# Second pass of a forward Fourier transform: each matmul of 128 rows and 192 columns against two of 64 rows and 96 columns

## The chip, the cores and the metric

The kernel runs on one core of one Trainium2 chip, as one launch. The metric is the device time of that core in microseconds (us). Columns, rows and loads below are those of TensorE, the matrix engine: a matmul first loads its stationary operand (the weights) into the array of 128 by 128 cells, as an instruction of its own, and then streams the columns of its moving operand through it; sums arrive in PSUM.

## The reference

The input x has 4 batches of 3072 positions with 256 features, all float32. Three layers follow one another:

```python
X = rfft(x, axis=1)                               # 1537 frequencies
Yr = Xr @ w_r - Xi @ w_i + b_r
Yi = Xr @ w_i + Xi @ w_r + b_i
Y  = soft threshold of Yr and of Yi at 0.01
y  = irfft(Y)                                     # "Fourier"
xk, xr = mixes of y with y one position earlier
y  = sigmoid(xr @ w_r2) * (relu(xk @ w_k)**2 @ w_v)  # 256 -> 1024 -> 256
h  = y @ w_in                                     # 256 -> 2048
out = (h * tanh(softplus(h))) @ w_out             # 2048 -> 256
```

The change lies in the first line, the forward transform.

## The kernel before, in words

**Precision.** TensorE works on float32r operands here. For float32 accuracy every operand is split in two parts, a high one (written by a copy with rounding, on ScalarE) and a low one (the difference, on VectorE); `split`, L71 to L77, does both, so that the casts of many tiles are recorded at L76 and the differences at L77. A product is then three matmuls into one PSUM group: high by high, high by low, low by high.

**Forward transform.** 3072 is taken as 96 by 32. The first pass, `s1` (L256 to L269), sums over 96 with weights `FC` of 96 by 96 and goes through DRAM (`scr1`), which turns the data. The second pass, `s2` (L298 to L310), sums over 32. Real and imaginary part of 32 positions are 64 rows, so a group of 128 rows holds two independent sums of 64 rows, s = 0 and s = 1, and the constant matrix `MC` (128 rows, 192 columns: minus imaginary, real, imaginary, 64 columns of each) is block diagonal: in each of its three parts of 64 columns the rows 0 to 63 have values in the first 32 columns only, and the rows 64 to 127 in the last 32 only.

**A unit of work.** There are 48 units u, 12 a batch (`NU`, `NG`). A unit has 2 groups e of 128 rows, and 256 features, which as two halves dh of 128 are the weights' columns: `s2(u)` issues 2 x 2 x 3 = 12 matmuls, each with a weight load of 128 rows by 128 columns out of `Ah` or `Al`, and 192 moving columns of `MC`. The output tile `s2p` has two banks of PSUM, one for each e, and there is one buffer of it. `s2_ev(u)` (L317 to L335) splits it into `Xh` and `Xl` in SBUF, 768 elements in each of 128 partitions (ScalarE L76, VectorE L77). `mix(u)` (L339 to L361) multiplies these with the layer's weights in 24 matmuls of 256 columns, adds the bias and applies the threshold on VectorE (L358 to L360). `is1(u)` (L369 to L379) is the first pass of the inverse transform, 3 matmuls of 512 columns (6 of 256 in four units).

**Order.** The program is ordered by hand; each engine carries out its instructions in the order written. The loop at L620 issues in turn u: `s2(u + 2)`, its eviction `s2_ev(u + 2)`, with `split_Y(u - 1)`, evictions of the first pass and two steps of background work (`bg`: splitting of later weights, mostly on VectorE) after it; the load of unit u + 5 from `scr1` (SP's queue) and the split of unit u + 4 into `Ah` and `Al`; the copy of the inverse pass's result (L388, to DRAM `scr2` by SP's queue); `mix(u)`; in 20 of the turns 12 matmuls of the first pass of a later batch; and `is1(u - 2)`. On TensorE a turn is thus: second pass, mix, first pass at times, inverse pass. From u = 33 on the next layer begins beside it (`early`, with matmuls of 96 rows and 128 columns, L458).

After this stage come the gated layer (from L819) and the last layer (from L1063), which the change does not touch.

Of the kernel before, what the change touches and what calls it, by code (L numbers as in the profile page):

```python
# [29 lines left out]
def kernel(  # L30
# [27 lines left out]
    nc = tc.nc  # L58
# [12 lines left out]
    def split(src, hi, lo, lo_eng=None, hi_eng=None):  # L71

        if hi_eng is nc.vector:
            nc.vector.tensor_copy(out=hi, in_=src)
        else:
            nc.scalar.copy(out=hi, in_=src)  # L76
        (lo_eng or nc.vector).tensor_tensor(out=lo, in0=src, in1=hi, op=ALU.subtract)  # L77
# [220 lines left out]
    def s2(u):  # L298
        last = u % NG == GS
        hl = Ah.pop(u)  # L300
        p = ps1p.tile([128, 2, 512], F32, tag="s2", name="s2p", bufs=1)
        for e in range(2):
            mc = MC[:, int(last and e == 1)]
            for dh in range(2):
                for i, (a, w) in enumerate(((0, 0), (0, 1), (1, 0))):
                    nc.tensor.matmul(  # L306
                        out=p[:, e, dh * 192:(dh + 1) * 192], lhsT=hl[a][:, e, dh * 128:(dh + 1) * 128],
                        rhs=mc[:, w, :], start=(i == 0), stop=(i == 2),
                    )
        s2_t[u] = p  # L310

    S1_AT = {2 + i: 4 + i for i in range(4)}
# [4 lines left out]
    def s2_ev(u, fill=lambda: None):  # L317
        last = u % NG == GS
        p = s2_t.pop(u)

        v = p[:, :, 0:384].rearrange("p e (h c) -> p e h c", h=2)
        xh = p1p.tile([128, 2, 2, 192], F32R, tag="Xh", name="Xh", bufs=3)
        xl = p1p.tile([128, 2, 2, 192], F32R, tag="Xl", name="Xl", bufs=3)
        split(v, xh, xl)
        fill()
        Xh[u] = (xh, xl)
        if last:

            xb = p1p.tile([128, 2, 2, 128], F32R, tag="Xb", name="Xb", bufs=1)
            for k, v in enumerate((xh, xl)):  # L330
                nc.scalar.copy(out=xb[:, k], in_=v[:, 1, :, 0:128])
            nc.scalar.activation(
                out=xb[:, :, :, 32:128:64], in_=xb[:, :, :, 32:128:64], func=AF.Copy, scale=0.0
            )
            Xb[u] = xb  # L335
# [204 lines left out]
    split_A(0)  # L540
    split_A(1)
    s2(0)
    s1(1, 2)
    split_mix(1)
    split_x(1, 3)
    s2_ev(0)
    s1_ev()
    s1_ev()
    s2(1)
    s1(1, 3)  # L550
    split_W()
    split_A(2)
    load_A(4)
    s2_ev(1)
    load_x(1, 5)
    split_x(1, 4)
# [6 lines left out]
    for h in range(2):  # L563
        for q in range(2):
            cs = slice(q * 512, (q + 1) * 512)
# [54 lines left out]
    for u in range(NU + 3):  # L620
        if u + 2 < NU:
            s2(u + 2)
# [3 lines left out]
        def fill():  # L626
            if 1 <= u <= NU:
                split_Y(u - 1)
            while s1_t:
                s1_ev()  # L630
            if u > 2:
                bg(2)

        if u + 2 < NU:
            s2_ev(u + 2, fill)
        else:
            fill()
# [11 lines left out]
        if u in S1_AT:  # L649
            i = 8 + S1_AT[u]  # L650
# [33 lines left out]
    for q in range(4):  # L684
        for h in range(2):
            cs = slice(q * 512, (q + 1) * 512)
# [132 lines left out]
    for t in range(NA + 1):  # L819
# [5 lines left out]
        for i2 in range(4):  # L825
# [48 lines left out]
            if t == NA - 1 and i2 == 0:  # L874
                hl = x2h_t[0] = w2p.tile([128, 2, 2, 512], F32R, tag="x2h", name="x2h", bufs=1)
# [292 lines left out]
```

## Time and profile before

| | us |
|---|---|
| median of 2 runs | 2007.81 (2006.71 to 2008.91) |
| span of the profiled execution | 2006.0 |
| TensorE busy in it | 1974.4 |
| VectorE busy | 1534.1 |
| ScalarE busy | 1149.5 |

The profiled execution's own time is its span, from the first to the last instruction; it lies 1.81 us under the median of the runs. The second pass runs from 37.6 to 301.6 us of it, 48 units, 576 matmuls. A matmul's recorded duration reaches from its start to its modelled end, and matmuls overlap in the pipeline: the pace is read from start to start. In a row of the timeline, "x2" with 0.36 us is two instructions of one group, from the start of the first to the end of the second.

### The profile page before, as it was taken

What the parts mean: (1) busy time and instruction counts of PE and PEld (TensorE: products, weight loads), DVE (VectorE), ACT (ScalarE), POOL (GpSimd) and SP (SyncE); (2) the same over time, 40 slices, a digit from 0 to 9 for tenths busy, and PEclk for the clock granted to TensorE, in tenths of its full rate; (3) what the DMA queues carried; (4) which work ended last, traced back from release to release, by engine and by line L of the source; (5) the groups of instructions that cost most, each with busy time, mean ns of one, the idle gap of its engine ahead of it and who ended that gap; (6) DMA issues with size and microseconds to landing.
All of it is one profiled execution on the core that took longest, in us unless ns stands there. A gap on an engine that the chain in (4) does not pass through costs nothing.

```text
span 2006.0 us, 33418 instructions
## 1 busy us (share of the span) xinstructions
PE 1974.4 (98%) x13284; PEld 1890.9 (94%) x13284; DVE 1534.1 (76%) x2487; ACT 1149.5 (57%) x1703; POOL 28.1 (1%) x45
## 2 busy tenths in 40 slices
PE   6999999999999999999999999999999999999998
PEld 5999999999999999999989999999999999999997
DVE  6899997777776776775587778777787777877775
ACT  6666656777777777776544444444444444544443
POOL 0000000000000000000000000000000000000000
PEclk8999999999999999999999999999999999999999
DMA  8676532112121211111101000001010010000000
GB/s 265 181 214 201 168 111 90 53 58 70 49 80 49 65 62 58 60 49 46 37 22 32 22 25 30 22 22 33 22 33 22 22 33 22 28 27 22 22 12 22
DMA packets 71501, 123.19 MB, mean 61 GB/s; under 512 B 6192, under 2 KB 48432, under 8 KB 71344
## 3 DMA queue, kind: packets, MB, share of 16 engines
q1 hardware_dynamic: 67200, 106.49, 18.0%
q0 software_dynamic: 4144, 14.55, 1.9%
q8 instruction: 105, 1.72, 0.4%
q14 instruction: 52, 0.43, 0.1%
HBM read 70.69 MB, written 50.33 MB: 60 GB/s over the span
## 4 chain that ended last, share of the span: by engine, by line
PE 91%; DVE 4%; DMA 2%; ACT 1%; issue 1%; SPq 0%; DVEq 0%; ACTq 0%
PE h L992 20%; PE o L1040 17%; PE kp L766 13%; PE vp L804 13%; PE o L1041 9%; PE mxp L352 5%; PE p L992 3%; PE pp L743 3%; PE pp L458 3%; PE s2p L306 2%; PE s1p L265 1%; PE i1p L376 1%; DMA XS<-in_x_dram 1%; DMA A<-scr 1%; DVE Xl L77 1%
## 5 line engine op out<-in xcount | busy, mean ns | idle before, releaser
L1040 PE MATMUL o<-WO,gh 128*128 128x512 f32 x1536 | 562.5, 395 | 0.0
L1041 PE MATMUL o<-WO,gl 128*128 128x256 f32 x1536 | 430.5, 280 | 0.0
L992 PE MATMUL h<-xS,WS 128*128 128x256 f32 x2208 | 351.6, 281 | 0.0
L1005 ACT COPY p1s<-p 128x256 f32<-128x256 f32 x184 | 68.9, 374 | 470.9 <-PE p L992 469.9
L1040 PEld LDWEIGHTS o<-WO,gh 128*128 128x128 f32 x1536 | 289.1, 188 | 43.3
L992 PEld LDWEIGHTS h<-xS,WS 128*128 128x128 f32 x2208 | 300.4, 189 | 16.1
L766 PE MATMUL kp<-xk,WK 128*128 128x384 f32 x1536 | 291.3, 338 | 0.3 <-DVE yT L474 0.3
L1041 PEld LDWEIGHTS o<-WO,gl 128*128 128x128 f32 x1536 | 289.8, 189 | 0.2
L804 PE MATMUL vp<-kh,WV 128*128 128x384 f32 x1024 | 281.7, 336 | 0.0
L766 PEld LDWEIGHTS kp<-xk,WK 128*128 128x128 f32 x1536 | 267.5, 189 | 0.8 <-ACT Cs L388 0.8
L995 DVE TENSOR_TENSOR C<-h,p1s 128x512 f32<-128x512 f32 x184 | 127.2, 691 | 161.7 <-PE h L992 161.7
L791 DVE TENSOR_TENSOR kl<-kr,kh 128x768 fp32r<-128x768 f32 x128 | 122.9, 960 | 163.6 <-ACT kr L790 163.3
L977 DVE TENSOR_TENSOR gl<-g,gh 128x1024 fp32r<-128x1024 f32 x184 | 223.7, 1216 | 2.1 <-ACT g L974 2.1
L973 ACT ACTIVATE gh<-C 128x1024 fp32r<-128x1024 f32 x184 | 195.7, 1063 | 11.0 <-DVE C L995 11.0
L974 ACT ACTIVATE g<-C 128x1024 f32<-128x1024 f32 x184 | 193.0, 1049 | 0.0
L992 PE MATMUL h<-xS,WI 128*128 128x256 f32 x1104 | 190.4, 280 | 0.0
L995 DVE TENSOR_TENSOR C<-h,wu 128x512 f32<-128x512 f32 x368 | 187.6, 552 | 0.1
L804 PEld LDWEIGHTS vp<-kh,WV 128*128 128x128 f32 x1024 | 186.7, 188 | 0.0
L804 PE MATMUL vp<-kl,WV 128*128 128x384 f32 x512 | 171.7, 335 | 0.0
L789 ACT ACTIVATE kh<-kr 128x768 fp32r<-128x768 f32 x128 | 108.4, 847 | 88.0 <-PE vp L804 87.9
L992 PEld LDWEIGHTS h<-xS,WI 128*128 128x128 f32 x1104 | 156.0, 189 | 0.2 <-DVE xS L953 0.2
L995 DVE TENSOR_TENSOR wu<-h,C 128x512 f32<-128x512 f32 x184 | 126.6, 688 | 35.0 <-PE h L992 31.1
(152 smaller groups left out, 3136.7 us busy)
## 6 DMA issues: line engine op xcount, KB each, us to landing
A<-scr SPq DMA_DIRECT2D x48, 256.0 KB
scr<-Cs SPq DMA_DIRECT2D x48, 256.0 KB
D<-scr SPq DMA_DIRECT2D x32, 384.0 KB
x2d<-r POOLq DMA_DIRECT2D x32, 384.0 KB, 3.5
x<-x2d SPq DMA_DIRECT2D x24, 512.0 KB
out_dram<-ob SPq DMA_DIRECT2D x96, 128.0 KB
scr<-st SPq DMA_DIRECT2D x27, 384.0 KB
xs<-in_x_dram SPq DMA_DIRECT2D x24, 384.0 KB
```

Of the source, the lines that this page charges most:

```text
L352: nc.tensor.matmul(out=p[:, e, :], lhsT=a, rhs=WX[:, dh, c, w, :], start=(i == 0), stop=(i == 11))
L766: nc.tensor.matmul(out=p[:, m, 0:TA], lhsT=WK[:, dh, w, f * 128:(f + 1) * 128], rhs=hl[:, v, dh, :], start=(i == 0), stop=(i == 5),)
L789: nc.scalar.activation(out=kh, in_=kr, func=AF.Square)
L791: nc.vector.tensor_tensor(out=kl, in0=kr, in1=kh, op=ALU.subtract)
L804: nc.tensor.matmul(out=p[:, o, 0:TA], lhsT=WV[:, f, w, o * 128:(o + 1) * 128], rhs=v[:, m, :], start=(f == 0 and i == 0), stop=(f == 7 and ...
L973: nc.scalar.activation(out=gh, in_=c, func=AF.Mish)
L974: nc.scalar.activation(out=g, in_=c, func=AF.Mish)
L977: nc.vector.tensor_tensor(out=gl, in0=g, in1=gh, op=ALU.subtract)
L992: nc.tensor.matmul(out=out, lhsT=a(l), rhs=xS[:, v, b, :], start=(n == 0), stop=(n == 2))
L995: nc.vector.tensor_tensor(out=out, in0=x0, in1=x1, op=ALU.add)
L1040: nc.tensor.matmul(out=o[m], lhsT=gh[:, m2, ms], rhs=WO[:, f], start=(f == 0), stop=False)
L1041: nc.tensor.matmul(out=o[m][:, 0, :], lhsT=gl[:, m2, ms], rhs=WO[:, f, 0, :], start=False, stop=(f == 15))
```

## The change

Each of the 12 matmuls of a unit becomes two. Matmul s takes rows 64 s to 64 s + 63 of the same weights (128 columns as before) and of `MC`, and from `MC` only the 96 columns in which those rows have values: 32 of each of the three parts, that is three runs of 32 with a step of 64. It thus lies in one half of the array's rows. The output of half s goes to bank s of `s2p` (before: bank e), with columns 192 e + 96 dh on. So the tile's order is now (s, then e, dh, part, 32 columns), and the eviction reads it back in the old order, 12 times 2 runs of 32, alternating between the banks. `Xh` and `Xl` and all that follows have the old layout. Values that are left out of the sums are products with zeros.

```diff
--- before.py
+++ after.py
@@ -303,10 +303,13 @@
             mc = MC[:, int(last and e == 1)]
             for dh in range(2):
                 for i, (a, w) in enumerate(((0, 0), (0, 1), (1, 0))):
-                    nc.tensor.matmul(
-                        out=p[:, e, dh * 192:(dh + 1) * 192], lhsT=hl[a][:, e, dh * 128:(dh + 1) * 128],
-                        rhs=mc[:, w, :], start=(i == 0), stop=(i == 2),
-                    )
+                    for s in range(2):
+                        rs, cs = slice(64 * s, 64 * s + 64), slice(192 * e + 96 * dh, 192 * e + 96 * dh + 96)
+                        nc.tensor.matmul(
+                            out=p[:, s, cs], lhsT=hl[a][rs, e, dh * 128:(dh + 1) * 128],
+                            rhs=mc[rs, w, :].rearrange("p (c s j) -> p c s j", c=3, s=2)[:, :, s, :],
+                            start=(i == 0), stop=(i == 2),
+                        )
         s2_t[u] = p
 
     S1_AT = {2 + i: 4 + i for i in range(4)}
@@ -318,10 +321,10 @@
         last = u % NG == GS
         p = s2_t.pop(u)
 
-        v = p[:, :, 0:384].rearrange("p e (h c) -> p e h c", h=2)
+        v = p[:, :, 0:384].rearrange("p s (c j) -> p c s j", c=12)
         xh = p1p.tile([128, 2, 2, 192], F32R, tag="Xh", name="Xh", bufs=3)
         xl = p1p.tile([128, 2, 2, 192], F32R, tag="Xl", name="Xl", bufs=3)
-        split(v, xh, xl)
+        split(v, *(a.rearrange("p e h (c s j) -> p (e h c) s j", c=3, s=2) for a in (xh, xl)))
         fill()
         Xh[u] = (xh, xl)
         if last:
```

## Rows read from the trace of the kernel before

**Rows 1.** The page: engines' busy time and share, instructions; a DMA queue: packets, MB, share.
```profile
span 2006.0 us, 33418 instructions
...
PE 1974.4 (98%) x13284; PEld 1890.9 (94%) x13284; DVE 1534.1 (76%) x2487; ACT 1149.5 (57%) x1703; POOL 28.1 (1%) x45
...
q8 instruction: 105, 1.72, 0.4%
```

**Rows 2.** The chain of waits, 0 to 400 us: share by line.
```profile
by line: PE mxp L352 23.9%; PE s2p L306 11.3%; PE s1p L265 7.2%; PE kp L766 7.2%; PE vp L804 6.0%; PE i1p L376 5.3%; DMA XS<-in_x_dram 3.4%; issue 2.9%; DMA A<-scr 2.6%; DVE Xl L77 2.5%; DMA xs<-in_x_dram 2.5%; DVE Al L77 2.3%; DVE yt L358 
```

**Rows 3.** Table by stretches: busy (instructions) of each engine, granted clock, DMA share, GB/s.
```profile
50.00:250.00 200.00, 200.00 (x1619) 195.93 (x1619) 188.16 (x293) 127.46 (x218) 0.00 (x0) 1.00 0.65 192
250.00:300.00 50.00, 48.24 (x377) 45.50 (x375) 48.25 (x88) 27.77 (x51) 0.00 (x0) 1.00 0.36 109
```

**Rows 4.** Timeline, matmuls, 155.3 to 157.3 us: start, duration, what, count.
```profile
155.61 0.36 PE L306 MATMUL s2p<-MC,Ah 128*128 128x192 f32 x2
155.81 0.28 PE L306 MATMUL s2p<-MC,Al 128*128 128x192 f32 x1
...
156.26 0.38 PE L306 MATMUL s2p<-MC,Ah 128*128 128x192 f32 x2
...
156.93 0.42 PE L352 MATMUL mxp<-WX,Xh 128*128 128x256 f32 x2
```

**Rows 5.** Timeline, weight loads of the same unit.
```profile
155.72 0.19 PEld L306 LDWEIGHTS s2p<-MC,Al 128*128 128x128 f32 x1
155.84 0.30 PEld L306 LDWEIGHTS s2p<-MC,Ah 128*128 128x128 f32 x2
...
156.84 0.30 PEld L352 LDWEIGHTS mxp<-WX,Xh 128*128 128x128 f32 x2
```

**Rows 6.** Timeline, weight loads, the unit at half clock; nine loads between these starts.
```profile
38.97 0.55 PEld L306 LDWEIGHTS s2p<-MC,Ah 128*128 128x128 f32 x2
...
40.89 0.28 PEld L265 LDWEIGHTS s1p<-xh,FC 96*96 96x96 f32 x1
```

**Rows 7.** Timeline, weight loads of the first pass: 22 us; and 153 us, after mix.
```profile
22.55 0.16 PEld L265 LDWEIGHTS s1p<-xh,FC 96*96 96x96 f32 x1 [0.79 <-ACT xh L76]
22.64 0.16 PEld L265 LDWEIGHTS s1p<-xl,FC 96*96 96x96 f32 x1
...
153.39 0.17 PEld L265 LDWEIGHTS s1p<-xh,FC 96*96 96x96 f32 x1
153.51 0.16 PEld L265 LDWEIGHTS s1p<-xl,FC 96*96 96x96 f32 x1
```

**Rows 8.** Groups by shape, 45 to 320 us: rows*columns, count, busy, mean ns, idle before.
```profile
L306 PEld LDWEIGHTS s2p<-MC,Ah 128*128 128x128 f32 x368 | 58.0, 191 | 7.4 <-DVE Xl L77 4.6
...
L77 DVE TENSOR_TENSOR Xl<-s2p,Xh 128x768 fp32r<-128x768 f32 x47 | 44.7, 952 | 4.3 <-ACT Xh L76 4.1
...
L265 PEld LDWEIGHTS s1p<-xh,FC 96*96 96x96 f32 x165 | 24.0, 162 | 0.0
...
L458 PEld LDWEIGHTS s1p<-ifh,Dl 96*128 96x128 f32 x16 | 3.1, 192 | 0.2
```

**Rows 9.** Timeline, matmuls, a unit that began after a wait.
```profile
250.98 0.47 PE L306 MATMUL s2p<-MC,Ah 128*128 128x192 f32 x2 [0.44 <-DVE Xl L77]
```

**Rows 10.** Groups by line, 0 to 700 us and 45 to 320 us: additions from PSUM.
```profile
L474 DVE TENSOR_TENSOR yT<-ya,pp 128x128 f32<-128x128 f32 x108 | 24.3, 281 | 0.0
...
L474 DVE TENSOR_TENSOR yT<-ya,s1p 128x64 f32<-128x64 f32 x24 | 3.7, 216 | 0.2 <-ACT ya L471 0.2
```

**Rows 11.** Waits, 0 to 320 us: us in total, times, longest.
```profile
ACT Xh L76 <- PE s2p L306: 71.6, 45, 3.4
```

**Rows 12.** Waits, 45 to 360 us, as above.
```profile
PEld s2p L306 <- DVE Xl L77: 4.6, 7, 0.9
```

## The prediction, made before the changed kernel was run

> **What bounds the kernel now.** I read the page first. TensorE is busy for nearly the whole span, while the lines of VectorE and ScalarE stay below it [rows 1]: a change on TensorE must be priced on TensorE. The chain of waits, cut to the first 400 us, shows who sets the end in the stage that holds the change: the matmuls of mix lead, those of the second pass (L306) stand second with 11.3%, and VectorE and DMA have a few per cent each [rows 2]. The table by stretches says the same of the steady part: between 50 and 250 us TensorE is busy without a break, at the full clock, and VectorE comes close to it; from 250 to 300 us TensorE lacks 1.8 us of 50 [rows 3]. So until 250 us every us added to TensorE's stream is added to the time, and later a few can vanish in gaps.
>
> Then the question is what a matmul of the second pass costs there, and the timeline answers it. The matmuls of a unit go by in about 0.11 us each, though 192 columns need less: the first two of a unit, whose weights were ready, last 0.36 us together where one lasts 0.28, so they follow one another in 0.08 to 0.09 us; a later pair takes 0.38 [rows 4]. The weight loads show why. From the third of the unit (155.72) to the first of mix (156.84) there are ten, in 1.12 us: **0.112 us each**, back to back [rows 5]. At half clock the same loads take 1.92/9 = 0.213 us each (38.97 to 40.89) [rows 6], and loads of 96 columns follow one another in 0.08 to 0.09 us where they run freely (22.55, 22.64) [rows 7]. The pace goes with the clock and with the number of weight columns. This pass is held by its **weight loads**, not by the columns that stream through.
>
> **The change, part by part.** *Streaming.* A matmul's 192 columns become two of 96, which may run beside each other. By the pace of the free pair, 0.085 us for 192 columns, that is 0.04 us for 96. But it was not the limit: worth nothing as long as a load takes 0.112 us.
>
> *Weight loads.* Each of the 12 loads of a unit becomes two, and each has 128 columns still; only its rows are halved. Do rows count? A load of 96 rows and 128 columns takes 192 ns, one of 128 rows and 128 columns 191, one of 96 by 96 162 [rows 8]: columns count, rows don't. The Trainium skill says so too (TensorE: Matmul & The Clock Gate, LDWEIGHTS): a load's time goes by its columns and not by the contraction rows; the trace agrees with the rows just named. So 12 loads more a unit. The trace has no load into half of the rows, and what a pair costs is bounded from two sides. One after another: 12 x 0.112 = 1.34 us a unit, 48 units, **64.5 us**. At the same time, in the two halves: nothing. A gain would need a load that is shorter for its fewer rows, which the 96-row loads speak against. I take the upper end: every load in the trace, whatever its shape, starts after its predecessor at the pace of its columns, and none starts beside another. One unit runs at half clock [rows 6]: 12 x (0.213 - 0.112) = 1.2 us more.
>
> *Issue.* The unit's 24 instructions on TensorE become 48. Their dispatch is not seen alone; 12 loads and 12 matmuls go by in the 1.32 us from 155.61 to 156.93 [rows 4], so one costs 0.055 us or less. At nothing it adds nothing. At that bound, 24 more cost 1.32 us, the price of the loads again, and not on top of it. A second way to the same sum.
>
> *Entering and leaving the half-array layout*, twice a unit, 96 times. The trace shows no such switch; between 96-row and 128-row instructions the loads go on without a pause (153.39 and 153.51) [rows 7], which gives zero for the lower end. The upper end is a full stop: the tail of a matmul beyond its slot, 0.27 - 0.11 = 0.16 us, and a weight load that nothing covers, 0.11, together 0.27 us, 26 us in all. The nearest row is a unit that began after a wait: its first two matmuls last 0.47 us [rows 9] instead of 0.36 [rows 4], 0.11 us for starting with no weights ready. I take that: 96 x 0.11 = **10.6 us**. The Trainium skill (TensorEngine Tiling, Key Properties) has a rule against this change: a switch of tiling mode drains TensorE. No run here shows it yet; by it the switches would cost up to the 26 us, without it nothing.
>
> *The evictions.* ScalarE's Xh and VectorE's Xl now read runs of 32 elements from two banks in turn. Additions that read PSUM in runs of 32 take 216 ns for 64 elements and 281 for 128 [rows 10], 1.02 ns an element, so 768 would be 0.93 us against the 952 ns of Xl now [rows 8]: no cost to be seen. A loss here is covered as well: ScalarE idles 71.6 us in all ahead of Xh, 45 times, waiting for the pass [rows 11], and the next unit needs the tile only after mix, some 3 us later. That s2p is one buffer matters only where VectorE is late.
>
> *What a later end of the pass sets back.* Behind Xh on ScalarE are queued Yh, the copies of st and Cs and the splits; behind Xl on VectorE are Yl and Al. All of them feed TensorE one or two units later, and TensorE itself is late by the same amount, so no new wait arises. No DMA is added or moved past another on SP's or POOL's queue; their triggers only come later with ScalarE's copies. The additional instructions, 1152 beside 33418, are 3% of a queue that takes 0.4% of the DMA engines [rows 1]: nothing.
>
> *What the gaps give back.* In the steady part TensorE's loads of this pass wait 4.6 us in 7 places for VectorE's Xl [rows 12]. VectorE gains 1.34 us a unit on TensorE, so these waits go: -4.6 us.
>
> **Sum:** 64.5 + 1.2 + 10.6 - 4.6 = +71.7 us. The profiled execution has a span of 2006.0 us; the median of the runs, 2007.8, is 1.8 us above it. 2006.0 + 71.7 + 1.8 = **2079 us**, +3.6%. With both ends of the switch cost (0 and 26 us), and 0 to 7 us given back, this case spans 2066 to 2096.
>
> **Rivals.** *The halves load side by side.* If the load into rows 64 to 127 starts while the one into rows 0 to 63 is under way, a pair takes the slot that one takes now, and the pass stays at 1.34 us a unit. The price is then the switches alone: 2008 us without one, 2018 with 0.11 us each, 2034 at the full stop: not slower by more than 2%. It decides at the second load of a pair: the loss falls below 40 us as soon as its start-to-start is less than half of 0.112 us, switches at my price. Against it: no two loads overlap in that way in this trace. For it: no load here names half of the rows, so the trace could not show it. The Trainium skill (TensorEngine Tiling, Key Properties) states this rule: tiles are independent, and different ones can load weights and multiply in parallel; no run here shows it yet. Chance 0.41.
>
> *Halved outright.* If a load into 64 rows cost half, or the halves hid each other's loads wholly, the pass would be held by streaming, 12 x 0.04 us beside each other: 0.83 us less a unit, 40 us, 1968 us; one half of that, 1988, is more believable. Against it are the loads of 96 rows. The Trainium skill (TensorEngine Tiling, Theoretical Speedup) gives up to 2x for a contraction of 64 or less; by that the pass would save 32 us. Nothing in this trace supports it for a pass held by weight loads. Chance 0.03.
>
> *The change does not take effect*: the 64-row matmuls occupy the whole array and run in a row. Then streaming adds nothing either, as 0.04 us stays under a load's 0.112: the forecast's 64.5 us without the switches, 2068. It lies within the forecast.
>
> **How the numbers follow.** Forecast, two slots for a pair, be it by loading or by dispatch: 0.56. Side by side 0.41, halved 0.03. About 2% (40 us, to 2048 or 1968) is what a measurement of this kernel can tell from no change. The forecast's case lies wholly above 2048, the second wholly within, the third almost wholly within: faster 0.01, within 2% 0.43, slower 0.56. The range must reach to the second case: 2008 to 2096 leaves out its lowest end, the third case and a switch dearer than a full stop, together some 0.15. The forecast's own range is 2066 to 2096.
>
> **What would show it.** In the changed kernel's timeline of weight loads, the second load of a pair starts 0.11 us after the first (forecast) or within some 0.06 us (side by side). A unit of the pass takes 2.7 us or 1.3 to 1.6. At the last matmul of is1 and the first of mix a pause of 0 to 0.27 us tells the switch. Xl should stay near 0.95 us, and the waits of loads for Xl should be gone. The prediction is wrong if the loads of the two halves overlap, if a load of 64 rows is clearly shorter than 191 ns, if the evictions slow down by tenths of a us, or if the clock of this stage falls below 1.00.

## The result and the profile after

The changed kernel takes 2023.1 us (2022.1 to 2024.2) against 2007.8, a ratio of **1.008** (95% interval 1.0064 to 1.0096). Run again beside the later experiments it took 2024.4 against 2007.3 (1.0086, 1.0072 to 1.0099). It is slower by 15 to 17 us, not by the 71 us of the forecast; the rival "the halves load side by side" had 2008 to 2034. Times are medians of executions with a mean granted clock of 0.98 or more; one execution of experiment 9, at 0.653, took 2770.9 us and is left out of its ratio.

The weight loads of one unit in the changed kernel, by the timeline (start, duration, what, count), answer to [rows 5]:

```profile
160.24 0.30 PEld L308 LDWEIGHTS s2p<-MC,Ah 64*128 64x128 f32 x4 [0.37 <-DVE yc L362]
160.46 0.19 PEld L308 LDWEIGHTS s2p<-MC,Al 64*128 64x128 f32 x2
...
161.47 0.19 PEld L308 LDWEIGHTS s2p<-MC,Al 64*128 64x128 f32 x2
```

Four loads last 0.30 us together, as long as two did before, and two last 0.19 us, as long as one. The two loads of a pair start within the resolution of a row (0.01 us), and a pair takes the slot of one. That holds for the whole unit: its 24 loads start between 160.24 and 161.47. The group by shape shows that a load of 64 rows is hardly shorter (its mean of 192 ns holds some loads at half clock; between 60 and 300 us, at the full clock, it is 187 against 191 before), and that VectorE's Xl costs what it did [rows 8] (count, busy, mean ns, idle before):

```profile
L308 PEld LDWEIGHTS s2p<-MC,Ah 64*128 64x128 f32 x744 | 57.5, 192 | 14.4 <-issue 2.8 <-DVE yt L363 1.8 <-DVE yt L361 1.8
...
L77 DVE TENSOR_TENSOR Xl<-s2p,Xh 128x768 fp32r<-128x768 f32 x47 | 44.8, 952 | 16.7 <-ACT Xh L76 16.7
```

The idle time before these loads has grown from 7.4 to 14.4 us, and the releasers are of every kind, some 0.37 us each, which is a sign that none of them is the cause: loading stands still at nearly every unit. The timeline of the matmuls around the unit shows the first place where time goes, beside [rows 4]; the line by itself is the matmul ahead of that unit in the kernel before:

```profile
159.92 0.40 PE L379 MATMUL i1p<-Yh,WC 128*128 128x512 f32 x1
160.25 0.42 PE L308 MATMUL s2p<-MC,Ah 64*128 64x96 f32 x4
160.51 0.28 PE L308 MATMUL s2p<-MC,Al 64*128 64x96 f32 x2
160.62 0.39 PE L308 MATMUL s2p<-MC,Ah 64*128 64x96 f32 x4
...
161.51 0.28 PE L308 MATMUL s2p<-MC,Al 64*128 64x96 f32 x2
161.72 0.50 PE L355 MATMUL mxp<-WX,Xh 128*128 128x256 f32 x2
```

```profile
155.38 0.39 PE L376 MATMUL i1p<-Yh,WC 128*128 128x512 f32 x1
```

From the last matmul of the inverse pass to the first of the unit it takes 0.33 us, where it took 0.23 in the kernel before (155.38 to 155.61); from the last pair (161.51) to mix it takes 0.21 us instead of 0.11; and the first matmuls behind either edge need longer too (0.42 us for the first four instead of 0.36 for the first two; 0.50 for mix's first two instead of 0.42 [rows 4]). A turn of the loop grows from 4.91 to 5.23 us, or from 6.32 to 6.65 where it holds a piece of the first pass: **0.32 us a unit, 0.16 a switch**.

The second place is the clock. The table by stretches, kernel before and then changed kernel, 25 to 50 and 50 to 75 us (the granted clock follows POOL's column):

```profile
25.00:50.00 25.00, 18.25 (x113) 16.65 (x112) 14.73 (x19) 16.73 (x28) 1.14 (x3) 0.73 0.76 260
50.00:75.00 25.00, 25.00 (x206) 24.56 (x206) 21.25 (x32) 15.76 (x28) 0.00 (x0) 1.00 0.63 168
```

```profile
25.00:50.00 25.00, 18.49 (x112) 16.31 (x110) 13.96 (x18) 14.53 (x24) 1.14 (x3) 0.56 0.76 262
50.00:75.00 25.00, 25.00 (x230) 23.63 (x228) 18.27 (x26) 12.35 (x19) 0.00 (x0) 0.89 0.42 101
```

The clock has two levels here, full (2.4 GHz) and half (1.2 GHz), so a mean of 0.73 is half clock for twice 0.27 of the 25 us: 13.5 us before. After the change it is 22 us and 5.5 more in the next stretch, some 27.5. Both kernels fall to half at 28 to 29 us, in the first pass, whose matmuls wait there up to 1.8 us at a time. The changed one stays there 14 us longer, although TensorE is busy without a break from 44 us on: three units of the second pass run at half clock instead of one.

Third, the gaps. The loads of the pass wait for Xl twice, where they did in 7 places [rows 12]; waits, 45 to 375 us:

```profile
PEld s2p L308 <- DVE Xl L77: 0.8, 2, 0.5
```

The sum, from the starts of units: the fifth unit begins at 60.97 us instead of 55.12, +5.85, of which four units' switches at 0.32 are 1.3; the remaining 4.5 are put down to the clock. Until the last unit, 43 turns at 0.325 us would add 14.0; the last begins 16.6 us late, so 3.3 us were given back, all in the last ten turns, in which the kernel before waits. From there on both kernels keep step, and the spans differ by 16.4 us (2022.4 and 2006.0).

### The profile page after: what moved, and what is told of

The parts are those of the page before. It is cut to its first block, busy times and chain, and to the rows that moved or that the text cites. A ratio compares the mean times of both kernels' runs of the same rounds, so it can differ in the third digit from the quotient of the medians.

```text
span 2022.4 us, 34570 instructions
## 1 busy us (share of the span) xinstructions
PE 1993.6 (99%) x13860; PEld 1897.6 (94%) x13860; DVE 1535.5 (76%) x2487; ACT 1148.4 (57%) x1703; POOL 28.1 (1%) x45
## 4 chain that ended last, share of the span: by engine, by line
PE 95%; DVE 2%; DMA 2%; ACT 1%; issue 0%; SPq 0%; DVEq 0%; ACTq 0%
PE h L995 19%; PE o L1043 17%; PE kp L769 13%; PE vp L807 13%; PE o L1044 9%; PE mxp L355 7%; PE s2p L308 4%; PE p L995 3%; PE pp L746 3%; PE pp L461 3%; PE s1p L265 2%; PE i1p L379 1%; DMA XS<-in_x_dram 1%; DMA xs<-in_x_dram 0%; PE h0p L712 0%
```

## The experiments

The theory after the result (**S**): loads into different halves run side by side, and the loss is the 96 switches and the longer half clock. The first four kernels ran on one chip, with the kernel before at 2007.0 us.

**1. All 192 columns for both halves.**

```diff
-  out=p[:, s, cs], rhs=mc[rs, w, :].rearrange(...)[:, :, s, :]
+  out=p[:, s, dh * 192:(dh + 1) * 192], rhs=mc[rs, w, :]
```

> Both halves stream all 192 columns, zeros included (the group e = 1 overwrites e = 0 in PSUM, so a part of the second pass is lost). Theory S, the loads of the two halves run side by side and the loss of the change is the 96 switches of layout plus a longer stretch at half clock: 192 columns need 0.085 us and still fit under a pair of loads of 0.112, so the time stays at that of the changed kernel, 2023 within 3 us. Theory T, the halves stream one after another and only 96 columns hide it: 2 x 0.085 = 0.17 us a pair, 12 x 0.06 x 48 = 33 us more, some 2056. Theory C, the longer half clock comes from the fewer columns streamed: 4 to 5 us less, some 2018.

Measured: 2024.7 us (ratio 1.009, 1.0076 to 1.0104). Four of its matmuls, of 192 columns, take 0.39 us, as four of 96 columns do in the changed kernel (160.62 above):

```profile
161.19 0.39 PE L308 MATMUL s2p<-MC,Ah 64*128 64x192 f32 x4
```

The halves stream side by side too, and the columns saved by the change are worth next to nothing (a turn of 5.27 us instead of 5.23), because loads hold the pass. The half clock lasted as long as in the changed kernel (0.57 and 0.89 in the two stretches), so it is not due to fewer columns.

**2. The loads doubled without the halves.** The kernel before, each matmul of the pass split into two of 96 columns and all 128 rows:

```diff
+  for s in range(2):
-    out=p[:, e, dh * 192:(dh + 1) * 192], rhs=mc[:, w, :]
+    out=p[:, s, (2 * e + dh) * 96:(2 * e + dh) * 96 + 96], rhs=mc[:, w, 96 * s:96 * s + 96]
```

> The kernel before with each matmul of the pass split into two of 96 columns, but each with all 128 rows: 12 weight loads more a unit, as in the change, without the halves. Theory S: loads into the same rows follow one another, 0.112 us each, 24 slots a unit: 64.5 us more, less some 5 us given back by waits for VectorE, 2062 to 2074. Rival D, the unit's loads never were the limit or the chip overlaps any two loads: no change, 2008 within 3 us.

Measured: 2074.6 us (1.0341, 1.0326 to 1.0355). Four loads take 0.53 us here, 0.19 + 3 x 0.112:

```profile
154.85 0.53 PEld L307 LDWEIGHTS s2p<-MC,Ah 128*128 128x128 f32 x4
```

A turn grows from 4.91 to 6.25 us, by 1.34. This is the forecast's price to the digit, for loads into the same rows. What the forecast priced exists; the change just doesn't pay it. This kernel writes the two banks of `s2p` in turn and reads them back in turn (in runs of 96), as the change does, and a turn pays for the 12 loads alone: the banks are not where the change's 0.32 us go. The time lies 0.6 us above the range expected; the half clock was longer here too (0.55 and 0.77 in the two stretches).

**3 and 4. One more matmul of the whole array, at the end or in the middle of the pass.** Its result is not used.

```diff
+  if e == 1:   # the other kernel: e == 0
+    nc.tensor.matmul(out=p[:, 0, 384:480], lhsT=hl[0][:, e, 0:128], rhs=mc[:, 0, 0:96], ...)
```

> One more matmul of 128 rows and 96 columns at the end of each unit's pass, just ahead of mix, so in the whole-array layout: no switch more. Theory S: 48 x 0.11 = 5 us over the changed kernel, 2028. Rival R, the loss of 0.32 us a turn comes from the doubled number of instructions and not from switches: 0.32/12 = 0.03 us for it, 1 to 2 us, 2025.

> The same additional matmul in the middle of the pass, between the groups e = 0 and e = 1: two switches of layout more in each unit. Theory S, 0.16 us a switch: 48 x 2 x 0.16 = 15 us over the kernel with it at the end, some 2043. Rival R, switches are free: the same time as with it at the end, within 2 us.

Measured: 2028.1 us at the end (1.0107, 1.0093 to 1.012), 2040.2 in the middle (1.0169, 1.0155 to 1.0183). The same instruction costs 12.1 us more where the layout must be left and entered again for it. In the middle:

```profile
163.06 0.27 PE L308 MATMUL s2p<-MC,Al 64*128 64x96 f32 x2
163.26 0.31 PE L314 MATMUL s2p<-MC,Ah 128*128 128x96 f32 x1
163.51 0.42 PE L308 MATMUL s2p<-MC,Ah 64*128 64x96 f32 x4
```

0.20 us to it and 0.25 us from it, in place of 0.11 each. Turns are 5.34 and 5.61 us: 0.13 us a switch. Switches cost, as S says; why 0.13 here and 0.16 at the unit's edges is not shown. The Trainium skill (TensorEngine Tiling, Key Properties) says that a change of tiling mode drains TensorE: the traces agree in that each change costs 0.13 to 0.16 us. Whether the array is empty in between they can't tell, as the ends of matmuls are modelled.

Experiments 5, 6, 8 and 9 ran on one chip, with the kernel before at 2007.3 us.

**5. The changed kernel again.**

> The changed kernel once more, as the reference of the runs beside it: 1.008 of the kernel before, some 2022 to 2024 us.

Measured: 2024.4 us (1.0086, 1.0072 to 1.0099), as above.

**6. The halves one after the other in each group of three.**

```diff
-  for i, (a, w) in enumerate(...):
-    for s in range(2):
+  for s in range(2):
+    for i, (a, w) in enumerate(...):
```

> The changed kernel with the three matmuls of half 0 first and those of half 1 after them, in each group of features. Theory S, only loads into different halves run side by side: the loads of one half follow one another at 0.112 us, and as one load at most is pulled ahead, 20 to 24 slots a unit in place of 12: 43 to 64 us over the changed kernel, 2066 to 2087. Rival L, the queue looks far ahead and brings the halves together whatever the order: 2023 within 3 us.

Measured: 2024.2 us (1.0085, 1.0071 to 1.0098), no change. S was too narrow: it held that the order of issue decides.

```profile
160.28 0.30 PEld L308 LDWEIGHTS s2p<-MC,Ah 64*128 64x128 f32 x4 [0.37 <-DVE yc L362]
160.50 0.20 PEld L308 LDWEIGHTS s2p<-MC,Al 64*128 64x128 f32 x2
```

The loads still come in pairs (two last 0.20 us, and four 0.30), although three of one half were issued ahead of the first of the other. As loads into one half follow one another at 0.11 us (experiment 7), the partners must be of different halves.

**7. The halves one after the other over the whole unit**, 12 and then 12 (the loop over s outermost).

> The changed kernel with all 12 matmuls of half 0 of a unit first and then the 12 of half 1. Three in front did not matter. Theory Q, the queue starts whatever half is free, over at least 12 loads and 12 matmuls in front: 2024 within 3 us, with the halves' loads some 0.04 us apart. Rival N, it sees only a few instructions ahead: the part of a half beyond that runs alone, up to 12 slots of 0.11 us a unit more, 2030 to 2087.

Measured: 2083.9 us (1.0382, 1.0365 to 1.04) beside 2007.3. The matmuls of a unit:

```profile
163.52 0.42 PE L308 MATMUL s2p<-MC,Ah 64*128 64x96 f32 x2
...
164.23 0.38 PE L308 MATMUL s2p<-MC,Ah 64*128 64x96 f32 x2
164.46 0.27 PE L308 MATMUL s2p<-MC,Al 64*128 64x96 f32 x1
164.46 0.49 PE L308 MATMUL s2p<-MC,Ah 64*128 64x96 f32 x4
164.72 0.34 PE L308 MATMUL s2p<-MC,Al 64*128 64x96 f32 x2
164.83 0.38 PE L308 MATMUL s2p<-MC,Ah 64*128 64x96 f32 x2
```

Eight matmuls go alone, 0.11 us each. As the ninth starts (164.46), the first of the other half starts too, over three that were issued before it; four of each half run side by side, and the last eight alone. Rival N holds: TensorE starts work for the free half over some three matmuls in front, not over twelve. That is 20 slots of 0.112 us instead of 12, 0.9 us more; a turn grew from 5.23 to 6.17 us, 45 us in 48 units. Most of the other 14 us go with the clock: between 76 and 376 us it was 0.95 on the mean, that is half clock for 30 us, where the changed kernel has 1.00.

**8. The first four units by whole matmuls.**

```diff
+  if u < 4:   # the loop of the kernel before, and its eviction
```

> The first four units, which run in the stretch in which the clock is at half, are computed by whole matmuls as before, the other 44 as in the change. Theory H, the switches at the start (0.3 us or more at half clock, 0.32 us a unit at full) bring about the longer half clock, 27 us in place of 14: the clock recovers as in the kernel before, and 1.3 to 2 us for switches and 4 for the clock are saved, some 2017. Rival P, the length of that stretch is the chance of the run: only the switches are saved, 2021 to 2022.

Measured: 2017.7 us (1.0055, 1.0042 to 1.0067), 6.7 us under the changed kernel beside it.

```profile
25.00:50.00 25.00, 17.77 (x101) 16.33 (x100) 14.36 (x19) 15.16 (x26) 1.13 (x3) 0.66 0.77 256
50.00:75.00 25.00, 25.00 (x238) 23.86 (x237) 20.60 (x30) 15.56 (x28) 0.00 (x0) 1.00 0.56 150
```

17 us at half clock; the changed kernel beside it had 0.57 and 0.82, some 30. Theory H has the time right: the longer stretch goes with the first four units, and the five executions (2017.2 to 2019.0) lie apart from those of the changed kernel (2022.0 to 2026.1), against rival P. What in these units does it is not told apart. Experiment 2, which has no switch, had 0.55 and 0.77, so it is not the switches alone, and experiment 1 excludes the columns.

**9. Every second unit by whole matmuls** (the same edit with `u % 2`).

> Every second unit by whole matmuls. Theory S: half of the switches, 24 x 0.32 = 7.7 us saved against the changed kernel, 2015 to 2016, and turns of 4.91 and 5.23 us (6.32 and 6.65) in alternation. Rival R, a unit's loss is due to something that lasts through the stage (clock, order of evictions): all turns are the same, or the loss is not halved.

Measured: 2012.0 us (1.0023, 1.0013 to 1.0033). The turns are 5.00 and 5.14 us, 6.42 and 6.55, on the mean 0.16 us over those of the kernel before: half of the loss, as S says, though each turn holds one edge of a halved unit, so they don't alternate between 4.91 and 5.23. The total fell further than expected, and the half clock was that of the kernel before in the two stretches (0.73 and 1.00), although units 0 and 2 were halved. What lengthens it thus stays open. No version tried beats the kernel before.

## Why the prediction was wrong

- *What bounds the pass*: right. Weight loads hold it, by columns and not by rows; a load of 64 rows takes 187 ns against 191 at the full clock, and 192 streamed columns in place of 96 changed next to nothing (experiment 1).
- ***Weight loads*: this is the step that failed.** It read "I take the upper end: every load in the trace, whatever its shape, starts after its predecessor at the pace of its columns, and none starts beside another". The rows were right and the inference was not: each of them went into rows that its predecessor had used too, so they could say nothing of two loads into different rows. The term of 64.5 us is 0: the second load of a pair starts within 0.01 us of the first, not 0.112 after it. The Trainium skill's rule on independent tiles (TensorEngine Tiling, Key Properties) speaks of exactly this case; the trace after agrees with it. Against its 0.41 stood only rows that could not bear on it.
- *Issue*: the bound of 0.055 us an instruction was far too high; 48 instructions go by in 1.47 us, 0.031 each, still held by loads.
- *Switches*: right in kind, too small. 0.16 us each and 15.5 us in all, against 0.11 and 10.6. The price was that of a start with no weights ready; what the other 0.05 us are, the tail of the matmul before or something else, no run tells apart.
- *Half clock*: sized at 1.2 us, for longer loads in one unit. The stretch itself grew by 14 us, worth some 4.5, and its cause stays open. The text named a lower clock as a sign of error and put no term to it.
- *Evictions, what is set back, gaps*: Xl 952 ns before and after; 3.3 us were given back instead of 4.6.

With the loads at 0 the forecast's own terms give 10.6 - 4.6 = 6 us more, 2014; with the measured switches, the clock and the gaps 15.5 + 4.5 - 3.3 = 16.7, against 16.4 between the spans; the terms are read from the same trace, so this is an account and no second proof. The range held the time because it reached down to the rival's case. The forecast's own case, 2066 to 2096, did not, and its loss was more than four times too large.

## What to carry to other kernels

Ask which of a matmul's two costs holds its slot, weight load or streaming: saving on the other one, here 96 of 192 streamed columns, bought nothing, however many zeros it left out. A trace in which each instruction shares rows of the array with the one before cannot tell what instructions in different halves do to one another; there a rule, or one small experiment, weighs more than the nearest row. Count the switches of layout, at 0.13 to 0.16 us each here, and set them against what a stretch in the other layout saves.

## What was not expected of the hardware

TensorE does not keep matmuls of different halves in the order of issue: a matmul of one half starts over some three earlier ones of the other (experiments 6 and 7). The Trainium skill (TensorE: Matmul & The Clock Gate, The mechanism) has matmuls in strict order of start and end, with weight loads alone pulled ahead. These traces differ, and the measurement decides: 24 loads in 12 slots with three of a half issued in a row.
